# Reordering the list of pieces in a fused attention and SiLU layer

## The chip, the cores and the metric
The kernel runs on one core of a Trainium2 chip. The metric is the device time of one execution in microseconds (us). The five engines that matter are the TensorE (PE, with its weight loads shown as PEld), the VectorE (DVE), the ScalarE (ACT), the GpSimd (POOL) and the SyncE (SP), which issues nearly all of the transfers.

## What the kernel computes
The input is a sequence of 2048 rows of 512. It is layer-normed once (xn), and the output is `x + A(xn) + B(xn)`:

```python
# A: 32 heads of 16, four segments of 512 rows, an additive memory M, z between segments
logits = einsum('bhqd,bhkd->bhqk', qs, ks) * scale + mask        # inside one segment
a_dot  = einsum('bhqk,bhkd->bhqd', softmax(logits), vs)
a_mem  = (phi(qs) @ M) / (phi(qs) . z + 1e-6)                    # phi(t) = t+1 if t>0 else exp(t)
o      = g * a_mem + (1 - g) * a_dot                             # then o @ wo
M, z   = M + phi(ks)^T vs, z + sum(phi(ks))
# B: a dense layer with 1792 hidden columns
out    = silu(xn @ w1) @ w2
```

## The kernel before
The kernel is one list of pieces, `ORDER`, written out by hand or by a search: 1349 words, each of which calls one small function (the dictionary `PIECES` at the end of the kernel). The functions are run in the order of the list, and no scheduler moves an instruction afterwards. So the list sets the order of instructions on each engine's own queue; each engine works through its queue in that order, and waits where an operand isn't ready. A word before another in the list is not finished before it: only the queues, the buffers and the data hold it back.

The words that this document uses (s is a segment, 0 to 3; a segment is four tiles of 128 rows):

- `X t.1`, `Xv`, `Xa`: the first transposes of normed rows on PE, and the copies of them to `xnT` on DVE or ACT. `XD t`: the same for later tiles, as a transposing transfer from SP. `xs t` are the sums of the layer norm on DVE (L286, L289), `xg` the roots on POOL, and `Nv t` the normed rows (L315, on DVE).
- `k s.dt.part`, `q s.dt.part`, `v s.j.part`, `h s.ft.part`: parts of the products for keys, queries, values and hidden columns, on PE (L336, or L338 where the product is made of four strips of 32 columns). In segments 0 and 1 a tile has four parts, afterwards two. `kv`, `qv`, `vv` copy the finished tile out of its PSUM bank on DVE (L376, L399, L406); `ka`, `qa` do it on ACT. `kp` and `kf` split the keys by heads. `ha` is the tanh of a hidden tile on ACT (L492) and `hv` the product that follows on DVE (L497); `hv` is what empties the bank.
- `S t`: the scores of a batch (L724), at once followed on ACT by their exponentials `Pb` (L730) and on POOL by the causal mask (L744). There are 72 of them, and all write the same four PSUM banks, `psS`. So the scores of one batch can start only when the exponentials of the batch before have ended.
- `E n`, `O n`: weights times values (L791), for the even and odd heads; `Ev`, `Ov`, `Om` copy and merge the results on DVE and send the row sums on by small transfers (L813).
- `s`, `sv`, `r`, `w`, then `z`, `d` (small transfers from SP, L577, that spread a row to 16 partitions), `zv`, `dv`, `n`, `nv`: the normalization, and the memory's part. `fp`, `fa`, `fv` and `gp`, `ga`, `gv` form phi of keys and queries, `t` turns it by a transfer, `m`, `mv`, `mw` add it to the memory.
- `o`, `oc`, `od`, `oh` are parts of the output products (full, half and quarter width, and halves of the last tile); `xl` loads a tile of x, `st` and `sh` add it and store.

PSUM is the point where the queues hold each other. Four banks are `psS`. The other four are one pool:

```python
pp = ctx.enter_context(tc.tile_pool(name="pp", bufs=4, space=bass.MemoryType.PSUM))
psatt = ctx.enter_context(tc.tile_pool(name="psatt", bufs=1, space=bass.MemoryType.PSUM))
...
def bank(shape, dtype, name):
    return pp.tile(shape, dtype, name=name, tag="pb")
```

Every tile of k, q, v, h, the weighted values, the memory and most of the outputs takes one of these four banks with its first product, keeps it until its reader on DVE or ACT is done, and the next tile waits for that. With all four taken, the first product of a new tile waits for one particular reader, and so for everything that stands ahead of that reader on its queue.

A last rule in the driver makes a word's products in one piece or in four strips, after what stands around it, so that PE changes its way of tiling seldom: a dense word between two `S` takes strips if the next tiled word is an `E` or `O`. The list therefore sets this too.

Of the kernel before, what the change touches and what calls it, by code (L numbers as in the profile page):

```python
# [16 lines left out]
ones0 ones1 zeros xc0 xd0 xc1 xq0 xi0 Nv0 busy44 xd1 xq1 xc2 busy6 xi1 X0.1 xd2 xq2 Nv1 X1.1 Xa0.1 v0.0.0 v0.0.1 v0.0.2 xs3 xi2 Nv2 xq3 xi3 v0.0.3 X2.1 Xa1.1 k0.1.0 tb Nv3 X3.1 Xv2.1 k0.1.1 Xv3.1 vv0.0 odd omask k0.0.0 k0.0.1 k0.0.2 k0.0.3 ka0.0 fp0.0 q0.0.0 kf0.0 q0.0.1 q0.0.2 q0.0.3 k0.1.2 k0.1.3 q0.2.0 v0.2.0 qa0.0 xs5 ka0.1 kp0.1  # L17
S0 v0.1.0 v0.1.1 xs6 xs7 q0.2.1 v0.2.1 v0.2.2 v0.2.3 vv0.2 fa0.0 k0.2.0 k0.2.1 k0.2.2 xs4 xg4.4
S2 q0.2.2 q0.2.3 qv0.2 k0.2.3 kv0.2 fp0.2 fa0.2 v0.1.2 v0.1.3 vv0.1 Nv5 Nv6 XD6 q0.1.0 q0.1.1 q0.1.2 q0.1.3 qv0.1
S1 h0.0.0 h0.0.1 h0.0.2 xs10 h0.0.3 v0.3.0 v0.3.1 v0.3.2 v0.3.3 ha0.0 vv0.3 q0.3.0 kp0.2 hv0.0  # L20
# [4 lines left out]
S11 hv0.4 q1.2.0 q1.2.1 q1.2.2 v1.3.1 kind fa0.1 q1.2.3 qv1.2 v1.3.2 v1.3.3 vv1.3 Nv8 XD8 O0 lw0 kp0.3 fv0.0 Ov0
S6 fa0.3 k1.2.0 k1.2.1 k1.2.2 h0.5.0 h0.5.1 h0.5.2 q1.1.0 h0.5.3 ha0.5 k1.2.3 kv1.2 q1.1.1 q1.1.2 hv0.5
S8 h0.7.0 q1.1.3 qv1.1 h0.6.0 h0.6.1 h0.6.2 h0.6.3 ha0.6 fv0.3 E1 Ev1 k1.0.0
S9 hv0.6 h0.7.1 h0.7.2 h0.7.3 Om0 ha0.7 k1.0.1 k1.0.2 kp1.2 q1.0.0 q1.0.1 q1.0.2 fp0.1 Nv9 XD9 xs12 k1.0.3 kv1.0 kp1.0
# [3 lines left out]
S15 h1.10.0 h1.10.1 h1.10.2 hv0.10 kp1.1 xl0.2 h1.0.3 ha1.0 Nv11 XD11 E2 Ev2 O2 Ov2
S17 h1.10.3 k1.3.0 hv1.0 k1.3.1 k1.3.2 k1.3.3 kv1.3 fp1.3 h0.12.0 h0.12.1 xs14 m0.2 mv0.2 ha1.10 h0.12.2
S21 fv0.1 q1.3.0 q1.3.1 q1.3.2 q1.3.3 qv1.3 h1.3.0 hv1.10 gp1.1 h0.12.3 ha0.12 t0.1 h1.3.1 h1.3.2 t0.0 h1.3.3
S14 hv0.12 k2.2.0 h0.11.0 h0.11.1 k2.2.1 h0.11.2 h0.11.3 xl0.0 h0.13.0 ha1.3
S16 ha0.11 h0.13.1 h0.13.2 kp1.3 h0.13.3 xs13 kv2.2 hv1.3 ha0.13 q2.1.0 q2.1.1 qv2.1 E3
S19 Ev3 h1.11.0 h1.11.1 h1.11.2 h1.11.3 hv0.11 O3 hv0.13 fa1.3 k2.1.0 mw0.2 k2.1.1 Ov3 kv2.1 Om2
# [905 lines left out]
```

## Time and profile before

| | before |
|---|---|
| median of 3 runs | 220.42 us (219.86 to 220.8) |
| profiled execution, from first to last instruction | 218.2 us |
| PE, ACT, DVE, POOL busy in it | 210.9, 184.1, 181.3, 127.4 us |
| granted PE clock | 1.000 |
| exponentials of the 72 batches | 135.2 us, 1.878 us each |

The page gives no time of the profiled execution other than its span; 2.2 us lie between the span and the median of the runs. In the views, a line has the start, the length, the engine, the line of the kernel, the operation and the tiles (out<-in) and, in brackets, how long the engine sat idle before it and what ended that. PE's records overlap, since products are pipelined: the distance from one start to the next is what a product costs, not its length. A few of PE's records are missing (3982 of 4006 products), and each leaves a gap as long as a product.

### The profile page before, as it was taken

To read this page: it belongs to the slowest core of one execution; us is meant where nothing else is said; L and a number is where in the kernel's file an instruction comes from. 1 tells how busy PE (TensorE), PEld (TensorE's weight loads), DVE (VectorE), ACT (ScalarE), POOL (GpSimd) and SP (SyncE) were. 2 spreads that over 40 slices of the span, in tenths; PEclk is the share of its full clock that TensorE was granted. 3 is DMA by queue.
4 is the path that set the end of the run, shared out by engine and by line. 5 is a ranking of instruction groups with operands and counts; after the bars stand their busy time and mean duration, and the time that the engine had idled before them with its cause. 6 is when DMAs were issued, how large, how long until landed. Compare 5 with 4: busy or idle time off the path is not lost.

```text
span 218.2 us, 9267 instructions
## 1 busy us (share of the span) xinstructions
PE 210.9 (97%) x3982; PEld 116.1 (53%) x4006; DVE 181.3 (83%) x370; ACT 184.1 (84%) x173; POOL 127.4 (58%) x203
## 2 busy tenths in 40 slices
PE   7899999999999999999999999999999999999994
PEld 7666656655544544455444545445464544465653
DVE  6899999999799899667979886887979897858844
ACT  3799999999999999999999999999989998942000
POOL 6067676789568984697766436962787473410000
PEclk9999999999999999999999999999999999999999
DMA  6996249322200430541125131420042120412223
GB/s 183 344 375 160 51 125 243 74 53 53 51 5 17 157 71 10 117 95 40 49 67 83 54 97 28 74 77 6 0 132 73 52 73 13 131 32 79 84 66 98
DMA packets 33273, 19.60 MB, mean 90 GB/s; under 512 B 14672, under 2 KB 33232, under 8 KB 33232
## 3 DMA queue, kind: packets, MB, share of 16 engines
q1 hardware_dynamic: 30608, 16.39, 28.7%
q10 hardware_dynamic: 2624, 2.62, 3.8%
q8 instruction: 31, 0.51, 1.0%
q14 instruction: 10, 0.08, 0.1%
HBM read 9.96 MB, written 2.10 MB: 55 GB/s over the span
## 4 chain that ended last, share of the span: by engine, by line
PE 92%; DMA 3%; ACT 2%; issue 1%; SPq 1%; DVE 0%
PE ps L336 26%; PE psO L338 17%; PE ps L338 16%; PE psS L724 11%; PE psO L336 9%; PE psV L791 8%; PE psS L338 4%; DMA wk_sb<-in_A_wk_dram 3%; ACT Pb L730 2%; PE psM L452 1%; SPq L169 0%; SPq L158 0%; PE ps L509 0%; ACT th L492 0%; DVE o_half L668 0%
## 5 line engine op out<-in xcount | busy, mean ns | idle before, releaser
L730 ACT ACTIVATE Pb<-psS 128x2048 bf16<-128x2048 f32 x72 | 135.2, 1878 | 4.7 <-PE psS L724 2.4
L744 POOL TENSOR_SCALAR_AFFINE_SELECT Pb<-Pb 128x512 bf16<-128x512 bf16 (+2 forms) x88 | 62.3, 718 | 22.4 <-ACT Pb L730 19.6
L497 DVE SCALAR_TENSOR_TENSOR hT<-th,ps 128x512 bf16<-128x512 bf16 x56 | 38.0, 682 | 10.1 <-ACT th L492 9.4
L744 POOL TENSOR_SCALAR_AFFINE_SELECT lows<-Pb 64x512 bf16<-64x512 bf16 (+1 forms) x40 | 24.3, 607 | 32.0 <-ACT Pb L730 24.9
L338 PE MATMUL psO<-w_sb,hT 128*32 128x512 bf16 (+2 forms) x696 | 41.4, 321 | 0.0
L336 PE MATMUL ps<-xnT,w_sb 128*128 128x512 bf16 (+1 forms) x177 | 35.9, 330 | 0.2 <-issue 0.2
L492 ACT ACTIVATE th<-ps 128x512 bf16<-128x512 f32 x56 | 33.0, 594 | 3.5 <-PE ps L338 3.1
L338 PEld LDWEIGHTS <-hT 128*32 128x32 bf16 x864 | 21.5, 96 | 14.6 <-issue 3.1
L338 PE MATMUL ps<-xnT,w_sb 128*32 128x512 bf16 (+1 forms) x408 | 24.8, 349 | 0.0
L724 PE MATMUL psS<-qT,k 32*128 32x64 bf16 (+3 forms) x512 | 23.0, 233 | 0.2
L336 PEld LDWEIGHTS <-w_sb 128*128 128x128 bf16 x178 | 16.4, 98 | 11.9 <-issue 1.2
L336 PE MATMUL psO<-w_sb,hT 128*128 128x512 bf16 (+2 forms) x82 | 20.5, 324 | 0.7 <-issue 0.6
L791 PEld LDWEIGHTS <-Vz 128*32 128x32 bf16 x768 | 16.1, 97 | 9.5 <-issue 0.6
L791 PE MATMUL psV<-Pb,Vz 128*32 128x448 bf16 (+7 forms) x512 | 21.0, 286 | 0.0
L724 PEld LDWEIGHTS <-k 32*128 32x128 bf16 x512 | 9.3, 92 | 21.2 <-issue 20.4
L336 PE MATMUL ps<-xnT,wk_sb 128*128 128x256 bf16 (+1 forms) x63 | 14.4, 326 | 0.4 <-DMA wk_sb<-in_A_wk_dram 0.2
L724 PE MATMUL psS<-qT,kT 16*128 16x448 bf16 (+3 forms) x256 | 14.7, 269 | 0.0
L338 PEld LDWEIGHTS <-w_sb 128*32 128x32 bf16 x408 | 10.3, 96 | 6.7 <-issue 1.7
L621 DVE SCALAR_TENSOR_TENSOR o_out<-psO,x_res 128x512 bf16<-128x512 f32 x14 | 9.4, 679 | 5.0 <-PE psO L338 3.9
L336 PEld LDWEIGHTS <-hT 128*128 128x128 bf16 x92 | 8.5, 98 | 9.6 <-issue 2.1
L828 DVE CAST odd<-psV 128x512 bf16<-128x512 f32 x16 | 11.0, 687 | 2.4 <-PE psV L791 2.4
L338 PE MATMUL psO<-wo_sb,oT 128*32 128x512 bf16 x140 | 12.8, 379 | 0.0
(112 smaller groups left out, 330.0 us busy)
## 6 DMA issues: line engine op xcount, KB each, us to landing
spr<-rz SPq DMA_DIRECT2D x56, 64.0 KB
x_res<-in_A_x_dram SPq DMA_DIRECT2D x16, 128.0 KB
out_dram<-o_out SPq DMA_DIRECT2D x15, 128.0 KB
w_sb<-in_B_w_dram SPq DMA_DIRECT2D x2, 896.0 KB
w_sb<-in_B_w_dram ACTq DMA_DIRECT2D x1, 1792.0 KB
x_hi<-in_A_x_dram SPq DMA_DIRECT2D x2, 512.0 KB
wv_sb<-in_A_wv_dram SPq DMA_DIRECT2D x2, 256.0 KB
wk_sb<-in_A_wk_dram SPq DMA_DIRECT2D x1, 512.0 KB
```

The lines of the kernel that those rows point to most:

```text
L336: return [nc.tensor.matmul(out, lhsT=lhsT, rhs=rhs, start=start, stop=stop, skip_group_check=True)]
L338: nc.tensor.matmul(out[c : c + 32], lhsT=lhsT[:, c : c + 32], rhs=rhs, start=start, stop=stop, tile_position=(0, c), skip_group_check=True,)
L452: nc.tensor.matmul(psM[32 * g : 32 * g + 32, i, :].rearrange("p (r d) -> p r d", d=DH), lhsT=st["phiK", dt][:, j, 32 * g : 32 * g + 32], r ...
L492: nc.scalar.activation(out=th[:], in_=sts[s]["h", ft][:, :], func=AF.Tanh, scale=0.5)
L497: nc.vector.scalar_tensor_tensor(out=st["hT"][:, ft, :], in0=st.pop(("th", ft))[:], scalar=1.0, in1=st.pop(("h", ft))[:, :], op0=ALU.add, ...
L621: out = nc.vector.scalar_tensor_tensor(out=o_out[:], in0=st.pop(("psO", j)), scalar=0.5, in1=st["x", j][:], op0=ALU.mult, op1=ALU.add)
L724: nc.tensor.matmul(psS[:, g, c : c + q2 - q1], lhsT=keys[rows], rhs=st["qT"][rows, dt, q1:q2], start=True, stop=True, tile_position=(32 * ...
L730: exp = nc.scalar.activation(out=blocks(Pb, b).rearrange("p y g c -> p g y c"), in_=psS[:, :, :].rearrange("p g (y c) -> p g y c", c=BLOCK ...
L744: over[id(Pb)].append(nc.gpsimd.affine_select(out=out, in_=in_, compare_op=ALU.is_ge, fill=0.0, base=base, pattern=[[0, out.shape[1]], [1, ...
L791: nc.tensor.matmul(psV[32 * g : 32 * g + 32, q0 : q0 + nq].rearrange("p (y c) -> p y c", y=weights.shape[2]), lhsT=Vzs[s % 2][:, kt, 4 * d ...
L828: copy(out=odd[:], in_=sts[s].pop(("psV", 1))[:, :])
```

## The change
The words of `ORDER` behind the first transposes stand in another order. The words are the same 1349, and loads, buffers and functions are unchanged; 21 more PE instructions come from seven products that are now made in four strips rather than in one piece. Three lines of the list, early in the first segment, show what the change looks like (whole lines of the list, as the diff has them):

```diff
-S2 q0.2.2 q0.2.3 qv0.2 k0.2.3 kv0.2 fp0.2 fa0.2 v0.1.2 v0.1.3 vv0.1 Nv5 Nv6 XD6 q0.1.0 q0.1.1 q0.1.2 q0.1.3 qv0.1
-S1 h0.0.0 h0.0.1 h0.0.2 xs10 h0.0.3 v0.3.0 v0.3.1 v0.3.2 v0.3.3 ha0.0 vv0.3 q0.3.0 kp0.2 hv0.0
...
+S2 v0.1.1 vv0.2 v0.1.2 q0.2.2 v0.1.3 q0.2.3 kp0.1 qv0.2 fa0.2 q0.1.0 Nv6 vv0.1 q0.1.1 q0.1.2 h0.3.0
+S1 h0.3.1 q0.3.0 h0.3.2 omask Nv7 fp0.1 Nv5 h0.0.0 h0.0.1 q0.1.3 Nv4 XD6 h0.0.2 qv0.1 h0.0.3 ha0.0
+S3 v0.3.0 v0.3.1 xs11 h0.3.3 ha0.3 v0.3.2 v0.3.3 kp0.2 q0.3.1 hv0.0 xs10 q0.3.2 q0.3.3 k0.3.0
```

The first place is PE's queue at the third and fourth of the first transposes (`xn_t` through `ident`, into `ptr`). Rows with a minus stood there before, rows with a plus stand there now:

```order
 L845 LDWEIGHTS xn_t
 L845 MATMUL ptr<-ident,xn_t 128x128
-L336 LDWEIGHTS wk_sb
-L336 MATMUL ps<-xnT,wk_sb 128x256
-L336 LDWEIGHTS wk_sb
-L336 MATMUL ps<-xnT,wk_sb 128x256
 L845 LDWEIGHTS xn_t
 L845 MATMUL ptr<-ident,xn_t 128x128
```

Two half-width products with the key weights `wk_sb` no longer stand between the third and the fourth transpose; they come behind the fourth.

The second place is DVE's queue early in the first segment, from the last sums of tiles 4 to 7 to the copy of the second query tile. Before (`ps_304`, `ps_301`, `ps_344`, `ps_327`, `ps_387` are v0.2, q0.2, k0.2, v0.1 and q0.1):

```order
L406 CAST Vz0_111<-ps_304 128x16x2x16
L286 BN_STATS stats_351<-x_hi_79 128x6
L289 BN_AGGR mv_all_140<-stats_351 128x2
L399 CAST qT_306<-ps_301 128x512
L376 CAST kT_281<-ps_344 128x512
L406 CAST Vz0_111<-ps_327 128x16x2x16
L315 TENSOR_SCALAR xn_t_382<-x_hi_79,mv_all_140,rstd_all_141 128x512
L315 TENSOR_SCALAR xn_t_384<-x_hi_79,mv_all_140,rstd_all_141 128x512
L399 CAST qT_306<-ps_387 128x512
```

Now, on the same queue (`ps_327`, `ps_296`, `ps_300`, `ps_341`, `ps_378` are k0.2, v0.2, q0.2, v0.1 and q0.1):

```order
L286 BN_STATS stats_338<-x_hi_79 128x6
L289 BN_AGGR mv_all_140<-stats_338 128x2
L376 CAST kT_277<-ps_327 128x512
L406 CAST Vz0_111<-ps_296 128x16x2x16
L399 CAST qT_306<-ps_300 128x512
L315 TENSOR_SCALAR xn_t_381<-x_hi_79,mv_all_140,rstd_all_141 128x512
L406 CAST Vz0_111<-ps_341 128x16x2x16
L235 CAST omask_130<-pm_odd_122 128x1
L315 TENSOR_SCALAR xn_t_420<-x_hi_79,mv_all_140,rstd_all_141 128x512
L315 TENSOR_SCALAR xn_t_424<-x_hi_79,mv_all_140,rstd_all_141 128x512
L315 TENSOR_SCALAR xn_t_433<-x_hi_79,mv_all_140,rstd_all_141 128x512
L399 CAST qT_306<-ps_378 128x512
```

All four sums of tiles 4 to 7 stand ahead of the first copy now, one normed tile stands ahead of the copy of v0.1, and four of them with the small `omask`, where there were two, ahead of the copy of q0.1.

The third place is the end of DVE's queue. Before:

```order
L621 SCALAR_TENSOR_TENSOR o_out_5531<-psS_4936,x_res_5420 128x512
L668 SCALAR_TENSOR_TENSOR o_half_5554<-psS_4936,x_res_5466 128x256
L621 SCALAR_TENSOR_TENSOR o_out_5577<-psO_5154,x_res_4186 128x512
L668 SCALAR_TENSOR_TENSOR o_half_5604<-psS_4936,x_res_5466 128x256
L938 UNCONDITIONAL_BRANCH
```

Now:

```order
L621 SCALAR_TENSOR_TENSOR o_out_5564<-psO_5210,x_res_5332 128x512
L668 SCALAR_TENSOR_TENSOR o_half_5599<-psS_4973,x_res_5522 128x256
L621 SCALAR_TENSOR_TENSOR o_out_5602<-psO_5105,x_res_4904 128x512
L668 SCALAR_TENSOR_TENSOR o_half_5625<-psS_4973,x_res_5522 128x256
L938 UNCONDITIONAL_BRANCH
```

The four last additions are the same; in the list the word `sh1` (the first `o_half`) now stands directly ahead of `st3.1`, with five narrow products behind the two, where before the list had three full and two narrow products between them.

More of the change, by code (lines that the diff above doesn't have):

```diff
@@ L32 @@
[L32 to L37, printed above, removed]
@@ new lines @@
+S1 h0.3.1 q0.3.0 h0.3.2 omask Nv7 fp0.1 Nv5 h0.0.0 h0.0.1 q0.1.3 Nv4 XD6 h0.0.2 qv0.1 h0.0.3 ha0.0
+S3 v0.3.0 v0.3.1 xs11 h0.3.3 ha0.3 v0.3.2 v0.3.3 kp0.2 q0.3.1 hv0.0 xs10 q0.3.2 q0.3.3 k0.3.0
+S4 qv0.3 XD7 XD4 XD5 k0.3.1 k0.3.2 h0.2.0 h0.2.1 hv0.3 vv0.3 h0.2.2 k0.3.3 v1.2.0 h0.2.3 h0.1.0 ha0.2
+S7 h0.1.1 h0.1.2 h0.1.3 v1.2.1 fv0.0 v1.2.2 ha0.1 xs9 kv0.3 hv0.2 v1.2.3 E0 vv1.2 Ev0
+S5 lw0 v1.1.0 xs8 h0.4.0 v1.1.1 fp0.2 hv0.1 v1.1.2 v1.1.3 h0.4.1 h0.4.2 v1.3.0 vv1.1 h0.4.3
+S11 q1.2.0 O0 kind q1.2.1 v1.3.1 fa0.1 v1.3.2 q1.2.2 Ov0 fv0.2 q1.2.3 kp0.3 v1.3.3 ha0.4
@@ new lines @@
+S12 k1.1.0 vv1.0 h0.10.2 Nv11 h0.10.3 k1.1.1 k1.1.2 k1.1.3 ha0.10 Om0 h1.0.0 h1.0.1 hv0.9 h1.0.2
+S15 kv1.1 XD8 hv0.10 E2 h1.10.0 tanh h1.10.1 Ev2 h1.10.2 XD11 kp1.1 h1.0.3 ha1.0 O2
+S17 h1.10.3 k1.3.0 Ov2 k1.3.1 h0.12.0 k1.3.2 hv1.0 m0.2 mv0.2 k1.3.3 h0.12.1 ha1.10 t0.0 kv1.3
+S21 h0.12.2 h1.3.0 h0.12.3 q1.3.0 q1.3.1 h1.3.1 hv1.10 gp1.1 h1.3.2 t0.1 mw0.2 ha0.12 h0.11.0 xs15 h1.3.3
+S14 ha1.3 h0.11.1 h0.11.2 q1.3.2 q1.3.3 hv0.12 qv1.3 k2.2.0 k2.2.1 h0.11.3
+S16 q2.1.0 q2.1.1 hv1.3 kv2.2 qv2.1 ha0.11 h0.13.0 h0.13.1 fp1.3 fa1.3 Om2 h0.13.2 E3 h0.13.3
@@ new lines @@
+S26 q2.0.0 od0.2.11.1 hv1.1 q2.0.1 oc0.0.7.1 h1.7.0 gp1.0 h1.7.1 h1.7.2 h1.7.3 qv2.0 ha1.7 oc0.2.5.1
+S23 h1.4.0 zv0.2 h1.4.1 gv1.2 hv1.7 h1.4.2 o0.2.16 o0.0.8 h1.9.0 h1.4.3 od0.2.11.3 o0.2.13 z0.0 zv0.3 ha1.4 h1.9.1
+S25 o0.2.12 kp2.1 Om1 hv1.4 h1.9.2 o0.2.3 o0.2.17 fp1.2 E5 h1.9.3 ha1.9 oc0.0.2.0 Ev5 zv0.0 hv1.9 o0.0.16
+S29 k2.3.0 k2.3.1 o0.2.14 oc0.2.5.0 h1.2.0 h1.2.1 fa1.2 kp2.0 o0.0.17 oc0.0.2.1
+S27 zv0.1 kv2.3 O5 o0.0.9 h1.2.2 o0.0.14 h1.2.3 o0.2.15 oc0.2.10.0 o0.2.9 Ov5 ha1.2
+S31 h1.13.0 st0.2 hv1.2 h1.13.1 h1.13.2 h1.13.3 o0.3.8 fv1.2 ha1.13 Om5 Nv12 o0.3.9 o0.0.4 o0.3.14 o0.3.16 od0.3.3.2
@@ new lines @@
+S41 fa1.1 hv1.5 o0.1.1 mw0.0 o0.3.12 v2.3.0 oc0.3.2.1 O7 Ov7 v2.3.1
+S37 o0.1.5 vv2.3 fv1.1 q3.3.0 od0.1.8.2 fp2.0 q3.3.1 o0.1.10 s1 od0.1.8.3 o0.3.13 t1.0 od0.3.3.1 qv3.3 ga2.3 Om6 od0.1.8.1
+S36 st0.1 o0.3.5 Om7 k3.1.0 t1.1 k3.1.1 sv1 ka3.1 q3.1.0 q3.1.1 r1.3 od0.3.3.3
+S40 h1.6.0 r1.1 h1.6.1 r1.2 r1.0 fv2.0 w1 h2.8.0 h1.6.2 h1.6.3 z1.2 z1.0 o0.3.4 ha1.6 gp2.3 h2.8.1 oc0.3.2.0 qv3.1
+S43 o0.3.7 hv1.6 o0.3.6 o0.3.15 m1.0 o1.2.8 mv1.0 kp3.1 oc0.3.0.0 d1.2 o1.2.7 E8 st0.3 ha2.8
+S38 Ev8 fa2.2 oc1.2.11.0 hv2.8 zv1.0 z1.1 fp2.2 v3.0.0 o1.2.13 k3.0.0 v3.0.1 k3.0.1
```

113 lines of the change are left out of this document (48 added, 65 removed).

## Prediction
> **What bounds the kernel now.** I read the page first, then what PE waited for, then busy time by stage, and at last the order of time where the change starts.
>
> ```profile
> span 218.2 us, 9267 instructions
> PE 210.9 (97%) x3982; PEld 116.1 (53%) x4006; DVE 181.3 (83%) x370; ACT 184.1 (84%) x173; POOL 127.4 (58%) x203
> ...
> PE psS L864 <- DVE zraw L188: 1.1, 1, 1.1
> PE psO L336 <- issue: 1.0, 6, 0.2
> PE ptr L845 <- DVE xn_t L315: 0.5, 1, 0.5
> ...
> 0.00:11.95 11.95, 10.04 (x96) 8.32 (x98) 8.70 (x26) 6.82 (x16) 4.24 (x16) 1.00 0.84 274
> 11.95:28.70 16.75, 16.45 (x208) 10.69 (x212) 16.25 (x35) 16.69 (x16) 11.91 (x19) 1.00 0.58 167
> 28.70:58.26 29.56, 29.34 (x589) 17.17 (x593) 27.51 (x59) 28.98 (x26) 22.23 (x36) 1.00 0.46 111
> ```
>
> PE is busy 97% of the span, and once the transposes are through it waits for almost nothing: the longest waits in its list belong to the first 7 us, and the "issue" gaps of 0.2 us are as long as one product, so they are missing records. The stage rows (PE, PEld, DVE, ACT, POOL) add the second point: from 11.95 to 28.70 us PE, ACT and DVE are all full, DVE with 16.25 of 16.75 us. There a new order has no slack to use; whatever stands badly on DVE's queue must reach PE.
>
> Against the median of 220.42 us the sum is made in differences to this execution; the 2.2 us between span and median are carried over unchanged.
>
> **PE's own work** does not change:
>
> ```profile
> 185.60 0.86 PE ps L336 x4
> ...
> 188.49 0.86 PE ps L338 x16
> ```
>
> Four full products in one piece take 0.86 us, and so do sixteen strips, which are four products: 0.215 us each either way. The words are the same, and PE changes into the score tiling 72 times in both lists. So seven more products in strips cost 0, from 0 to +0.1.
>
> **The start** is the one place that gains.
>
> ```profile
> 7.96 0.41 DVE L315 TENSOR_SCALAR xn_t<-x_lo,mv_all,rstd_all 128x512 bf16<-128x512 bf16 x1
> 8.54 0.39 PE L336 MATMUL ps<-xnT,wk_sb 128*128 128x256 bf16 x2 [0.24 <-DMA wk_sb<-in_A_wk_dram]
> 8.77 0.39 PE L845 MATMUL ptr<-ident,xn_t 128*128 128x128 bf16 x4
> 9.19 0.42 DVE L851 COPY xnT<-ptr 128x512 bf16<-128x512 bf16 x1 [0.43 <-PE ptr L845]
> 10.11 1.04 PE L336 MATMUL ps<-xnT,wq_sb 128*128 128x256 bf16 x8
> 10.30 0.58 ACT L376 CAST kT<-ps 128x512 bf16<-128x512 f32 x1 [0.58 <-PE ps L336]
> 10.92 0.51 ACT L393 ACTIVATE k<-kT,pm_even 128x256 bf16<-128x256 bf16 x1
> 11.34 0.56 ACT L399 CAST qT<-ps 128x512 bf16<-128x512 f32 x1
> 11.95 0.21 PE L724 MATMUL psS<-qT,k 32*128 32x64 bf16 x4
> ```
>
> The fourth transpose stood behind key products that waited for `wk_sb` until 8.54. Now it needs only its normed tile, ready at 8.37 (7.96 + 0.41): it starts at 8.41, the key products follow at 8.64, and `xnT` is whole at 9.25 (0.42 to its copy, 0.42 for it). k0.0 ends after five quarter-tiles of 0.216 at 9.72, where it ended at 10.11. ACT's chain (10.30, 10.92, 11.34) moves with it: keys at 9.91, queries at 11.05 (q0.0 ends at 10.80, and a copy starts some 0.25 later), done at 11.61. PE has the same eleven quarter-tiles before the first scores and comes at 11.67. S0 starts at 11.68 instead of 11.95: **-0.27**, between 0 (if `wq_sb` lands only when it was first used, 10.11) and -0.35.
>
> **DVE's queue behind it** takes more than that away.
>
> ```profile
> 11.51 0.69 DVE L286 BATCH_NORM_STATS2 stats<-x_hi 128x6 f32<-128x512 bf16 x1 [0.23 <-DMA x_hi<-in_A_x_dram]
> 13.13 0.66 DVE L286 BATCH_NORM_STATS2 stats<-x_hi 128x6 f32<-128x512 bf16 x1
> 13.93 0.66 DVE L406 CAST Vz<-ps 128x512 bf16<-128x512 f32 x1
> 14.50 0.69 DVE L286 BATCH_NORM_STATS2 stats<-x_hi 128x6 f32<-128x512 bf16 x1
> 15.32 0.69 DVE L399 CAST qT<-ps 128x512 bf16<-128x512 f32 x1
> 15.93 0.68 DVE L376 CAST kT<-ps 128x512 bf16<-128x512 f32 x1
> 16.53 0.68 DVE L406 CAST Vz<-ps 128x512 bf16<-128x512 f32 x1
> 17.13 1.18 DVE L315 TENSOR_SCALAR xn_t<-x_hi,mv_all,rstd_all 128x512 bf16<-128x512 bf16 x2
> 18.22 0.68 DVE L399 CAST qT<-ps 128x512 bf16<-128x512 f32 x1
> ...
> 20.80 0.41 DVE L315 TENSOR_SCALAR xn_t<-x_hi,mv_all,rstd_all 128x512 bf16<-128x512 bf16 x1
> 22.01 1.88 ACT L730 ACTIVATE Pb<-psS 128x2048 bf16<-128x2048 f32 x1
> 23.93 0.40 PE L724 MATMUL psS<-qT,k 32*128 32x64 bf16 x8
> ```
>
> Starts give the prices: a pair of sums 0.82 (14.50 to 15.32), a copy 0.60, a normed tile 0.545 ((18.22 - 17.13) / 2). The queue can't start before `x_hi` lands at 11.51, and this transfer is not moved. In the new order: four pairs of sums to 14.75; k0.2, v0.2, q0.2 to 16.56; one normed tile and v0.1's copy from 17.11, ended at 17.79; `omask` and three normed tiles; q0.1's copy from 19.41 to 20.10.
>
> PE on its side needs banks. A batch of scores takes 0.39, and the next cannot start before 2.38 (0.45 to the exponentials, 1.88 for them, 0.05 back: 22.01 + 1.88 to 23.93). So S2 is at 14.06 and S1 at 16.44. Three quarter-tiles behind S1, at 17.48, h0.0 takes the bank of v0.1, which is freed at 17.82: it waits 0.34. Of this only 0.08 counts, since this stage has eight quarter-tiles (2.12 us) and would have waited for the exponentials; S3 is at 18.90. Directly behind S3, at 19.29, v0.3 takes the bank of q0.1, freed at 20.13: **0.84** (0.45 if the normed tiles cost 0.41 each, 1.0 if q0.1 slips further). Nine quarter-tiles later S4 starts at 22.08, against 21.55 in the trace. Its stage waits 0.1 for q0.3's copy, and S7, S5 and S11 follow at 24.52, 26.90 and 29.28. The trace has S11 at 28.70: +0.58. With a last wait of 0.1 at O0 for v1.1's copy I take **+0.65** at S6, the start's gain included; bounds +0.1 and +1.1.
>
> **Score stages further on.** A stage below 2.38 us of PE work waits for exponentials. The new list has 2.15 between S17 and S21 (seven quarter-tiles, one memory product, the scores): +0.23. Two short stages of the old list (2.33 ahead of S31 and 2.36 ahead of S40, by the same count of products) are full in the new one: -0.07. **+0.16**, 0 to +0.3.
>
> **Banks that come back late.** I counted, in both lists, first products that take a bank within 1.31 us of the last product of its former tile, where one DVE copy lies between: 21 now, 10 before. A copy needs about 1.05 (0.35 to start, 0.69), so each holds only if DVE is idle at that moment. At 0 to 0.1 us for each of the eleven more, and little for most: **+0.2**, 0 to +0.8.
>
> **The end.**
>
> ```profile
> 214.44 0.69 DVE L621 SCALAR_TENSOR_TENSOR o_out<-psO,x_res 128x512 bf16<-128x512 f32 x1 [0.17 <-PE psO L338]
> 214.98 0.28 PE L338 MATMUL psS<-wo_sb,oT 128*32 128x256 bf16 x4
> 215.31 0.42 DVE L668 SCALAR_TENSOR_TENSOR o_half<-psS,x_res 128x256 bf16<-128x256 f32 x1 [0.18 <-PE psS L338]
> ```
>
> The last addition starts 0.33 behind the last product. Now a half addition (0.42) and a full one (0.69) run back to back ahead of it; they start 0.81 before the last product and end 0.33 behind it. They just fit, and the full tile's store goes out some 0.2 later: **+0.05**, 0 to +0.2.
>
> Sum: 0.65 + 0.16 + 0.2 + 0.05 = +1.06, so 220.42 + 1.06 = **221.5 us**.
>
> **The rivals.** A measurement of this kernel tells 0.5% (1.1 us) from no change.
>
> *x_hi lands early* (no change, 0.17). The 11.51 is one execution's landing. If the sums start at 10.9, when DVE is free, the chain is 0.6 earlier, h0.0 waits for nothing, v0.3 waits 0.24, and S11 comes at about 28.65: -0.05 + 0.16 + 0.1 + 0.05 gives 220.7. Against it: DVE's wait for the transfer is in the trace.
>
> *Small transfers were the cost* (faster, 0.07). If the timed runs have waits for late `spr` rows on the path that the profile has off it, the new list can remove them.
>
> ```profile
> DVE oT L589 <- DMA spr<-rz: 0.9, 2, 0.5
> ```
>
> With these 0.9 us, the start's 0.27 and the 0.07 above all gained, and no late bank, it gives 219.2. It decides from the point where such a wait of DVE holds PE; in the trace PE has none behind it, and the first spread, z0.2, is now read after 4.9 us of PE work where it was 7.7.
>
> *Transfers with too short a lead* (slower, 0.08). The list issues d2.2 2.6 us of PE work before it is read (7.5 before), and the transpose of tile 12 3.4 us before q3.3 (23.6 before). Each late by 0.6 (an estimate: the wait for `spr` above is 0.5 each) adds 1.2: 222.7.
>
> *POOL holds DVE's normed tiles* (slower, 0.08).
>
> ```profile
> 17.53 0.63 POOL L417 TENSOR_SCALAR pos<-kT 128x512 bf16<-128x512 bf16 x1
> 22.86 0.38 DVE L315 TENSOR_SCALAR xn_t<-x_hi,mv_all,rstd_all 128x512 bf16<-128x512 bf16 x1
> ```
>
> The two normed tiles at 17.13 took 1.18 beside this work of POOL, the one at 22.86 took 0.38. If each of the three tiles ahead of q0.1 waits out one POOL instruction (0.63) and then takes 0.38, they cost 1.01 each instead of 0.545: +1.4, 222.9. Against it: the two in the trace cost less than 2 x 1.01. The Trainium skill's page "SBUF — State Buffer", section "Who interferes with whom", states such a rule: a DVE tensor_scalar in a two-port mode and a GpSimd instruction exclude each other for the whole instruction. By that rule the sum would be this rival's 222.9, by the row it is 221.5; the trace agrees that the two disturb each other, but shows 0.21 more per tile (1.18/2 - 0.38) and not a whole POOL instruction.
>
> **How the numbers follow.** The sum's case has 0.60; its own range is 220.7 to 222.4, since most of its unknowns only add, and a little over half of it (0.34) lies beyond 221.5. So slower by over 0.5% has 0.34 + 0.16 = 0.50; within 0.5% has 0.26 + 0.17 = 0.43; faster has 0.07. The range that leaves out the faster case and the upper parts of the two slow rivals is 220.1 to 222.8.
>
> **What would show it.** S0 near 11.7 us. On PE a wait of some 0.8 us for DVE's copy of q0.1 (L399) directly behind the fourth batch of scores, and a shorter one before it for L406. S11 near 29.3. A wait for Pb of about 0.2 at S21. PE's busy time stays near 211 us. I am wrong if v0.3's first product follows S3 without a gap, or if PE waits for a transfer in the later segments.

## The result, and the profile after

| | before | after |
|---|---|---|
| median of six runs | 220.40 us | 226.75 us |
| ratio, with 95% interval | 1 | 1.0285 (1.0258 to 1.0312) |
| profiled execution, its span | 218.2 us | 224.6 us (run time 226.35) |

One of the six runs after, 229.98 us, was in the chip's slower state and is not in the ratio; the median of the other five is 226.36 us. The new order is 6.3 us slower, outside the range of 220.1 to 222.8 that was forecast. On the page of the kernel after, the span, the busy time of the engines and the shares of the chain that ended last:

```profile
span 224.6 us, 9318 instructions
...
PE 215.2 (96%) x4027; PEld 116.2 (52%) x4027; DVE 182.0 (81%) x370; ACT 184.2 (82%) x173; POOL 127.9 (57%) x203
...
PE 64%; DVE 15%; issue 6%; DMA 4%; POOL 4%; ACT 3%; SPq 2%; DVEq 0%; ACTq 0%; POOLq 0%
```

The same line of shares on the page of the kernel before:

```profile
PE 92%; DMA 3%; ACT 2%; issue 1%; SPq 1%; DVE 0%
```

Busy times hardly differ: DVE has 0.7 us more, ACT 0.1. (PE's 4.3 more are mostly records: 24 are missing before and none after. The old list without masks, experiment e7 below, has all 4006 records and 214.2 us, so some 3.3 are records.) But the chain, which ran over PE for 92%, now goes over DVE for 15% and over POOL for 4%. PE waits for them. The seven longest waits behind 12 us in the list of PE's waits after (us, count, mean):

```profile
PE ps L338 <- DVE qT L399: 0.8, 1, 0.8
PE ps L336 <- DVE hT L497: 0.5, 1, 0.5
PE ps L338 <- DVE oT L608: 0.5, 1, 0.5
PE ps L336 <- DVE qT L399: 0.5, 1, 0.5
PE ps L338 <- DVE oraw L821: 0.4, 1, 0.4
PE ps L336 <- DVE omask L235: 0.4, 1, 0.4
PE psV L791 <- POOL Pb L744: 0.3, 1, 0.3
```

Where the loss arises is seen from the starts of some batches of scores (rows of L724) in the two traces:

| | S0 | S6 | S19 | S36 | S59 | S71 | last product | end |
|---|---|---|---|---|---|---|---|---|
| before, us | 11.95 | 31.21 | 58.26 | 104.88 | 161.65 | 189.99 | 214.98 | 218.24 |
| after, us | 11.90 | 32.08 | 59.72 | 108.08 | 166.90 | 196.27 | 220.83 | 224.64 |
| difference | -0.05 | +0.87 | +1.46 | +3.20 | +5.25 | +6.28 | +5.85 | +6.40 |

It grows up to S71; only 0.87 us of it lies in the first stretch, on which the prediction had spent most of its working.

For the rest I went through PE's starts. Behind 12 us, the new list has 18 places where the distance from one start to the next is over 0.06 us longer than that pair of products needs elsewhere. They make 6.15 us; the old list has four, 0.46 us. (Missing records are left out.) Two early ones make 1.13: h0.0 at 18.26, v0.3 at 20.34. Five late ones make 3.39: O4 at 73.71, h1.9 at 79.74, v2.3 at 103.98, q3.0 at 124.56, v3.1 at 140.03. Eleven between 0.07 and 0.27 make 1.63.

The longest, 0.96 us, shows the kind. PE, DVE and POOL of the kernel after around it:

```profile
123.55 0.24 PE L338 MATMUL psO<-w_sb,hT 128*32 128x128 bf16 x4
124.56 0.62 PE L338 MATMUL ps<-xnT,wq_sb 128*32 128x512 bf16 x8 [0.78 <-DVE qT L399]
```

```profile
120.92 0.69 DVE L497 SCALAR_TENSOR_TENSOR hT<-th,ps 128x512 bf16<-128x512 bf16 x1 [1.05 <-ACT th L492]
121.52 1.10 DVE L599 TENSOR_TENSOR phiQT<-spr,phiQT 128x512 bf16<-128x512 bf16 x1
122.55 0.41 DVE L472 TENSOR_TENSOR Mbf<-M,bmask 128x256 bf16<-128x256 f32 x1
122.88 0.50 DVE L479 TENSOR_TENSOR Zw<-b,z 128x16 bf16<-128x16 f32 x2
123.28 0.63 DVE L589 TENSOR_TENSOR oT<-spr,oraw 128x512 bf16<-128x512 bf16 x1
123.83 0.68 DVE L399 CAST qT<-ps 128x512 bf16<-128x512 f32 x1
```

```profile
121.25 1.09 POOL L744 TENSOR_SCALAR_AFFINE_SELECT Pb<-Pb 128x1024 bf16<-128x1024 bf16 x1
122.84 0.80 POOL L744 TENSOR_SCALAR_AFFINE_SELECT Pb<-Pb 128x256 bf16<-128x256 bf16 x2 [0.50 <-ACT Pb L730]
```

q3.0 takes the bank of q3.2. Its reader is the copy at 123.83, and three words stand ahead of it on DVE: dv1.2, mw1.2 (two kinds of rows) and zv1.2. The second thing to see is their length. dv1.2 (L599) takes 0.42 where POOL is idle, here 1.10: it began while a causal mask ran on POOL from 121.25 to 122.34, and ended 0.28 behind that mask's end.

That is the rule in both traces. Of the L589 and L599 that began with over 0.15 us of a POOL instruction still to run, 19 of 20 ended 0.27 to 0.28 behind its end, however much was left of it. (In the one exception, before, the two began within 0.01 us of each other, and POOL's instruction was the longer one: 0.89 instead of 0.61.) All 12 of L315 that began with over 0.26 us to run ended 0.14 to 0.15 behind it. The copies out of PSUM (L399, L406, L821) take 0.63 to 0.69 with and without POOL. I call this a hold. Over all of DVE's instructions that can be held (L315, L433, L468, L472, L479, L550, L589, L599, L835), the time above the unheld kind is 8.7 us before and 11.2 after (to some 0.5, by which unheld length is taken).

### The profile page after: what moved, and what is told of

Same layout as the page of the kernel before. It is cut to its first block, busy times and chain, and to the rows that moved or that the text cites. A ratio compares the mean times of both kernels' runs of the same rounds, so it can differ in the third digit from the quotient of the medians.

```text
span 224.6 us, 9318 instructions
## 1 busy us (share of the span) xinstructions
PE 215.2 (96%) x4027; PEld 116.2 (52%) x4027; DVE 182.0 (81%) x370; ACT 184.2 (82%) x173; POOL 127.9 (57%) x203
## 4 chain that ended last, share of the span: by engine, by line
PE 64%; DVE 15%; issue 6%; DMA 4%; POOL 4%; ACT 3%; SPq 2%; DVEq 0%; ACTq 0%; POOLq 0%
PE ps L336 17%; PE psO L338 13%; PE ps L338 11%; PE psS L724 7%; PE psV L791 6%; PE psO L336 5%; DMA x_hi<-in_A_x_dram 3%; PE psS L338 3%; DVE phiQT L599 2%; ACT Pb L730 2%; DVE hT L497 2%; POOL Pb L744 2%; DVE phiQT L433 1%; ACT th L492 1%; DVE oT L589 1%
## 5 line engine op out<-in xcount | busy, mean ns | idle before, releaser
L338 PE MATMUL psO<-w_sb,hT 128*32 128x512 bf16 (+2 forms) x704 | 45.3, 326 | 0.0
L336 PE MATMUL ps<-xnT,w_sb 128*128 128x512 bf16 (+1 forms) x177 | 38.5, 330 | 1.1 <-DVE hT L497 0.5
L338 PE MATMUL ps<-xnT,w_sb 128*32 128x512 bf16 (+1 forms) x412 | 26.1, 349 | 0.0
L724 PE MATMUL psS<-qT,k 32*128 32x64 bf16 (+3 forms) x512 | 23.0, 233 | 0.1
L336 PE MATMUL psO<-w_sb,hT 128*128 128x512 bf16 (+2 forms) x90 | 22.0, 320 | 0.0
L724 PEld LDWEIGHTS <-k 32*128 32x128 bf16 x512 | 9.2, 92 | 20.8 <-issue 20.1
L336 PE MATMUL ps<-xnT,wk_sb 128*128 128x512 bf16 (+1 forms) x67 | 14.9, 329 | 0.0
L724 PE MATMUL psS<-qT,kT 16*128 16x448 bf16 (+3 forms) x256 | 14.7, 269 | 0.0
L338 PE MATMUL psO<-wo_sb,oT 128*32 128x512 bf16 x156 | 14.4, 380 | 0.1
L336 PE MATMUL ps<-wv_sb,xnT 128*128 128x512 bf16 x42 | 12.7, 380 | 0.5 <-DVE qT L399 0.5
```

Of the source, the lines that this page charges most:

```text
L336: return [nc.tensor.matmul(out, lhsT=lhsT, rhs=rhs, start=start, stop=stop, skip_group_check=True)]
L338: nc.tensor.matmul(out[c : c + 32], lhsT=lhsT[:, c : c + 32], rhs=rhs, start=start, stop=stop, tile_position=(0, c), skip_group_check=True,)
L724: nc.tensor.matmul(psS[:, g, c : c + q2 - q1], lhsT=keys[rows], rhs=st["qT"][rows, dt, q1:q2], start=True, stop=True, tile_position=(32 * ...
```

## The experiments

The table has the waits of PE behind 12 us in the profiled execution, counted as above, and the sum of DVE's lengthening. Each kernel was timed against the kernel before on the same chip (medians 220.1 to 220.5); three have a single run, and so no interval. In the profiled execution of e1 the products between 25 and 28 us took about twice as long as elsewhere (0.21 for a half-width product of 0.108), so its waits aren't summed.

| kernel | median, us | ratio (95%) | PE's waits, us | DVE longer by, us |
|---|---|---|---|---|
| before | 220.4 | 1 | 0.46 | 8.7 |
| after | 226.75 | 1.0285 (1.0258 to 1.0312) | 6.15 | 11.2 |
| e1, early words moved | 228.43 | 1.0377 (1.0320 to 1.0435) | - | 12.2 |
| e2, late words moved behind | 225.31 | 1.0210 (1.0166 to 1.0253) | 4.68 | 10.3 |
| e3, e1 and e2 | 226.10 | 1.0283 (1.0213 to 1.0353) | 5.61 | 10.8 |
| e4, new list to S6, then the old | 222.75 | 1.0098 (1.0062 to 1.0134) | 3.34 | 9.0 |
| e5, three words in the old list | 222.04 | 1.0080 (1.0057 to 1.0103) | 1.92 | 10.1 |
| e6, after without masks | 223.34 | single run | 2.58 | 3.5 |
| e7, before without masks | 220.61 | single run | 0.35 | 2.2 |
| e8, late words into idle time | 225.47 | 1.0237 (1.0182 to 1.0293) | 3.12 | 9.2 |
| e9, e8 with the old head | 225.15 | 1.0206 (1.0157 to 1.0255) | 4.12 | 7.9 |
| e10, e5 without masks | 220.49 | single run | 0.52 | 2.5 |
| e11, e8 with XD12 earlier | 224.64 | 1.0197 (1.0169 to 1.0225) | 3.90 | 8.6 |
| e12, e9 with XD12 earlier | 223.26 | 1.0135 (1.0104 to 1.0166) | 3.06 | 8.4 |

**First theory: each wait is the price of one misplaced word.** Then a move of a few words takes it away.

```diff
-S2 ... q0.1.0 Nv6 vv0.1 q0.1.1 q0.1.2 h0.3.0
-S1 h0.3.1 q0.3.0 h0.3.2 omask Nv7 fp0.1 Nv5 h0.0.0 h0.0.1 q0.1.3 Nv4 XD6 h0.0.2 qv0.1 h0.0.3 ha0.0
+S2 ... q0.1.0 vv0.1 Nv6 q0.1.1 q0.1.2 h0.3.0
+S1 h0.3.1 q0.3.0 h0.3.2 fp0.1 h0.0.0 h0.0.1 q0.1.3 XD6 h0.0.2 qv0.1 omask Nv7 Nv5 Nv4 h0.0.3 ha0.0
```

> The new list, with five words of DVE moved in its first 21 us: the normed tile Nv6 behind the copy vv0.1, and omask, Nv7, Nv5, Nv4 behind the copy qv0.1. In the trace of the new list h0.0 waits 0.56 us for vv0.1's bank at 18.26 and v0.3 waits 0.57 us for qv0.1's bank at 20.34. Theory A (each stall is the price of one word that stands ahead of a bank's reader on DVE): both go, 226.7 - 1.1 = 225.6, between 225.3 and 226.0. Rival B (the queue behind is as full, and the late normed tiles or late copies give the time back further on): over 226.3. Rival C (the loss is in small transfers that come late): no change.

It became slower, 228.4, and its interval lies clear of the new list's. Both early waits are gone, and a longer one stands behind them. DVE and PE of this kernel:

```profile
19.93 2.23 DVE L315 TENSOR_SCALAR xn_t<-x_hi,mv_all,rstd_all 128x512 bf16<-128x512 bf16 x3
22.08 0.68 DVE L286 BATCH_NORM_STATS2 stats<-x_hi 128x6 f32<-128x512 bf16 x1
22.79 0.18 DVE L289 BATCH_NORM_AGGREGATE mv_all<-stats 128x2 f32<-128x6 f32 x1
22.89 0.66 DVE L497 SCALAR_TENSOR_TENSOR hT<-th,ps 128x512 bf16<-128x512 bf16 x1
```

```profile
23.60 0.38 PE L336 MATMUL ps<-xnT,wk_sb 128*128 128x256 bf16 x2 [1.57 <-DVE hT L497]
```

The three normed tiles took 1.51 in the new list. Here the last of them meets a mask, they take 2.23, and PE waits 1.73 us for the next bank's reader, the product of h0.0. Rival B holds in this stretch: its queue has no free time.

```diff
-S18 ... xl0.0 kv2.0
-S22 o0.0.3 v2.2.0 ga1.0 h1.1.0 xg12.4 h1.1.1 ...
+S18 ... xl0.0 kv2.0 xg12.4
+S22 o0.0.3 v2.2.0 ga1.0 h1.1.0 h1.1.1 ...
...
-S23 h1.4.0 zv0.2 h1.4.1 gv1.2 hv1.7 h1.4.2 ...
+S23 h1.4.0 zv0.2 h1.4.1 hv1.7 gv1.2 h1.4.2 ...
...
-S34 ... vv2.0 gv1.3 E7 XD12 ha1.5 o0.1.7 oc0.1.9.0 Ev7
+S34 ... vv2.0 E7 XD12 ha1.5 o0.1.7 oc0.1.9.0 Ev7 gv1.3
...
-S39 ... q3.2.0 dv1.2 v3.3.0 mw1.2 zv1.2 q3.2.1 qv3.2 v3.3.1 ...
+S39 ... q3.2.0 dv1.2 v3.3.0 q3.2.1 qv3.2 mw1.2 zv1.2 v3.3.1 ...
...
-S49 ... od1.0.1.0 dv1.0 o1.0.16 n1.1 o1.0.0 nv1.1 o1.0.3
+S49 ... od1.0.1.0 o1.0.16 n1.1 o1.0.0 nv1.1 dv1.0 o1.0.3
```

> The new list, with six words moved at five places behind 60 us: xg12.4 ahead of S22, gv1.2 behind hv1.7, gv1.3 behind Ev7, mw1.2 and zv1.2 behind qv3.2, dv1.0 behind nv1.1. The trace of the new list has PE waiting there 0.46, 0.69, 0.58, 0.96 and 0.70 us, 3.4 together. Theory A: nearly all of it goes, 226.7 - 3.1 = 223.6, between 223.2 and 224.3. Rival B (a queue without slack: what is moved behind makes the next reader late): less than half goes, over 225.2. Rival C (transfers): no change.

> The eleven moves of the two runs before together. Theory A: the two gains add, 222.5, between 222.0 and 223.2; what is left over the kernel before is the dozen of waits under 0.3 us. Rival B: the gains overlap or turn into new waits, over 224.5.

Of the 3.4 us, 1.4 came back in the time. The first two of the five waits are gone, the other three were replaced by waits of 0.54, 0.66 and 0.34 and a new one of 0.21. At q3.0's place, on DVE and PE of e2:

```profile
123.52 0.84 DVE L589 TENSOR_TENSOR oT<-spr,oraw 128x512 bf16<-128x512 bf16 x1
124.28 0.68 DVE L821 CAST oraw<-psV 128x512 bf16<-128x512 f32 x1
```

```profile
125.01 0.62 PE L791 MATMUL psV<-Pb,Vz 128*32 128x448 bf16 x16 [0.48 <-DVE oraw L821]
```

zv1.2, moved behind the copy of q3.2, now stands ahead of the next bank's reader, and is held there (0.84 instead of 0.41). e3 adds the early moves to this; its median is 0.8 above e2's, but the intervals of the two ratios overlap. The first theory falls: a word's move pays only where the queue behind it has room.

**The head alone, and one bad place alone.**

The first kernel is a splice: the new list up to S6, then the old list's words in their order. At the seam the words that the new head has already run (fp0.1) are left out, and those that it has not run yet (tanh of xg8.4, fp0.3, hv0.4, qv1.2, vv1.3, Nv8, XD8) are put in. The second kernel moves three words in the old list.

> The new list up to S6 (its first 185 words), then the remaining words in the old order. It prices alone the stretch for which the prediction worked out +0.65 us, and which in the two traces costs +0.87 (S6 at 32.08 against 31.21). Theory A: 220.4 + 0.87 = 221.3, between 221.0 and 221.6. Rival B (the old list further on has slack that takes the delay up): 220.4 to 220.8. Rival D (a bad head also makes the rest worse, since DVE stays behind): over 222.

222.75: rival D, by its bound of 222. Besides the 0.87 up to S6, PE waits 0.60 at 33.66 and 0.46 at 36.73, directly behind the seam, where DVE is still behind. A further 0.80 at 177.99 follows a wait of DVE of 0.9 us for a late `spr` row in this execution (0.5 in the trace before); without it the time would be near 222.0, at that bound, so this run alone does not decide for D. The times lie between 221.9 and 223.4.

```diff
-S42 ... vv3.0 zv1.1 gv2.3 o1.2.4 fp2.2 zv1.2
-S39 hv2.11 q3.2.0 ga2.1 q3.2.1 qv3.2 d1.0 v3.3.0 ...
-S44 dv1.2 q3.0.0 q3.0.1 Ev9 mw1.0 oc1.2.3.1 ...
+S42 ... vv3.0 zv1.1 gv2.3 o1.2.4 fp2.2
+S39 hv2.11 q3.2.0 ga2.1 q3.2.1 dv1.2 mw1.0 zv1.2 qv3.2 d1.0 v3.3.0 ...
+S44 q3.0.0 q3.0.1 Ev9 oc1.2.3.1 ...
```

> The old list with three words moved: dv1.2, mw1.0 and zv1.2 now stand directly ahead of the copy qv3.2 on DVE, as the like words do in the new list at its longest stall (0.96 us, q3.0 waiting for the bank of q3.2). Nothing else changes. Theory A (one such order is enough, in a list with no other fault): +0.5 to +1.0, 220.9 to 221.4. Rival B (the old list's slack takes it up; the stalls need a list that is behind everywhere): within 0.2 of 220.4.

222.04, 1.9 us above the kernel before on that chip: more than theory A's upper end. One wait arises, of 1.45 us, at q3.0. DVE and PE:

```profile
117.33 0.69 DVE L497 SCALAR_TENSOR_TENSOR hT<-th,ps 128x512 bf16<-128x512 bf16 x1 [0.52 <-ACT th L492]
117.93 1.09 DVE L599 TENSOR_TENSOR phiQT<-spr,phiQT 128x512 bf16<-128x512 bf16 x1
118.95 0.83 DVE L472 TENSOR_TENSOR Mbf<-M,bmask 128x256 bf16<-128x256 f32 x1
119.70 0.47 DVE L479 TENSOR_TENSOR Zw<-b,z 128x16 bf16<-128x16 f32 x2
120.08 0.62 DVE L589 TENSOR_TENSOR oT<-spr,oraw 128x512 bf16<-128x512 bf16 x1
120.63 0.68 DVE L399 CAST qT<-ps 128x512 bf16<-128x512 f32 x1
```

```profile
121.36 0.83 PE L338 MATMUL ps<-xnT,wq_sb 128*32 128x512 bf16 x12 [1.38 <-DVE qT L399]
```

**Order or hold.** The same kernels without most of the masks tell the two apart.

```diff
-            over[id(Pb)].append(nc.gpsimd.affine_select(
+            (nc.gpsimd.affine_select(
...
-            for first in chunks:
-                select(first[:, :, 0:HP], first[:, :, 0:HP], HP)
             return
...
-        select(firsts[:, :, 0:P], firsts[:, :, 0:P], 0)
```

The first pair of lines stops the remaining masks from being put on the list of what later exponentials wait for.

> The new list without the causal masks of the weights Pb (the 88 POOL instructions Pb<-Pb of L744 are left out, so the weights above the diagonal aren't zeroed; those that fill lows stay). In the trace of the new list the DVE instructions that read and write bf16 tiles in SBUF (L315, L433, L589, L599, L835 and a few more) are 11.2 us longer together than their shortest kind, 6.7 of it while such a mask runs. Theory E (DVE instructions of this kind are held until POOL's is through, and these held ones make the bank's reader late): L599 and L589 beside nothing fall to 0.42, the 11.2 fall to about 4.5, and the time by 2.5 to 3.5 us, to 223.2 to 224.2. Rival F (the order of words alone makes the reader late, the holds fall in slack): the time falls by under 1 us.

> The old list without the same 88 masks. Here 8.7 us of lengthened DVE instructions, 6.4 of them beside such masks, reach PE nowhere. Theory E: DVE's busy time falls by 5 to 6.5 us and the time by under 0.4, to 220.0 to 220.5. Rival F: the same small change; it differs from E only in the new list.

> e5_one_bad (three words moved in the old list, one stall of 1.45 us) without the same 88 causal masks as in the two kernels without masks. In e5 the words between hv2.11 and the bank's return took 1.09, 0.83, 0.47, 0.62 and 0.68 us; at their shortest (0.42, 0.41, 0.28, 0.41, 0.68) the copy would end 1.4 us sooner. Theory E (the stall is mostly the hold by POOL): a stall of 0 to 0.4 at this place. Rival F (the order alone): 1.0 or more.

The new list falls by 3.0 to 3.4 us (by the median of the five runs or of all six) to 223.34, the old one doesn't fall (220.61), and the one bad place costs nothing any more (220.49). DVE and PE of e10, at the same place (line numbers behind the edit are 3 smaller):

```profile
117.80 0.69 DVE L497 SCALAR_TENSOR_TENSOR hT<-th,ps 128x512 bf16<-128x512 bf16 x1 [0.58 <-ACT th L492]
118.40 0.64 DVE L599 TENSOR_TENSOR phiQT<-spr,phiQT 128x512 bf16<-128x512 bf16 x1
118.97 0.41 DVE L472 TENSOR_TENSOR Mbf<-M,bmask 128x256 bf16<-128x256 f32 x1
119.30 0.27 DVE L479 TENSOR_TENSOR Zw<-b,z 128x16 bf16<-128x16 f32 x2
119.47 0.41 DVE L589 TENSOR_TENSOR oT<-spr,oraw 128x512 bf16<-128x512 bf16 x1
119.81 0.68 DVE L399 CAST qT<-ps 128x512 bf16<-128x512 f32 x1
```

```profile
120.54 0.83 PE L338 MATMUL ps<-xnT,wq_sb 128*32 128x512 bf16 x12
```

The order is that of e5 word for word; the copy begins 2.01 us behind the start of hv2.11 instead of 3.30, and the wait falls from 1.45 to 0.17. So at this place the hold is nearly all of the price.

In the whole of the new list PE's waits fall from 6.15 to 2.58, but this is not the hold alone, because the masks also stand in POOL's own queue. Of the five long waits, three have held DVE instructions ahead of the late reader (h1.9, q3.0, v3.1; 2.35 us together). O4 (0.46) waits for a mask itself, and v2.3 (0.57) stands behind a DVE instruction that waited for a result of POOL:

```profile
102.63 0.69 DVE L433 SCALAR_TENSOR_TENSOR phiQT<-ex,pos 128x512 bf16<-128x512 bf16 x1 [1.65 <-POOL pos L417]
```

That L417 began at 101.99, directly behind masks in POOL's queue; in e6 this wait of DVE is gone. How the 3.6 us divide between the hold and POOL's queue is measured only at q3.0's place. Nor are the 2.58 that remain the order's alone: 1.05 of them stand where DVE idled 1.32 us for a late `spr` row (178.94), a place that costs 0.26 in the new list's profile. Without this wait and the 0.35 of the old list without masks, about 1.2 us are left for the order, beside the masks that e6 keeps (its DVE is still lengthened by 3.5). The Trainium skill's page "SBUF — State Buffer", section "Who interferes with whom", states that a DVE instruction with two SBUF inputs contends with a GpSimd instruction that reads SBUF, and that the order of issue decides which of the two blocks. The trace agrees: the later L599 ends 0.27 behind POOL's instruction.

**Moves into idle time.** Before hv2.11 DVE sat idle for 1.05 us (the row at 120.92), and for 0.65 before hv2.12. Words moved there go ahead of the bank's reader without delaying it. Besides the first two moves of e2 (xg12.4 and gv1.2):

```diff
-S39 gv2.3 hv2.11 ... dv1.2 ... mw1.2 zv1.2 q3.2.1 qv3.2 ...
+S39 gv2.3 dv1.2 mw1.2 hv2.11 ... q3.2.1 qv3.2 ...
...
+S44 ... Ev9 zv1.2 q3.0.0 ...
+S46 ... dv1.0 hv2.12 ...
+S41 fa1.1 hv1.5 gv1.3 ...
```

> The new list with the five late places mended in another way than in e2_late_mended: words go where the trace of the new list has DVE idle, ahead of the bank's reader, or behind every reader that PE needs soon. xg12.4 ahead of S22 and gv1.2 behind hv1.7 as there; gv1.3 behind hv1.5 (not between Ev7 and it); dv1.2 and mw1.2 ahead of hv2.11 (DVE idle 1.05 us before it); zv1.2 behind Ev9; dv1.0 ahead of hv2.12 (idle 0.65 before it). Theory G (DVE has free time near each place, and what is moved into it costs nothing): 226.7 - 3.0 = 223.7, between 223.3 and 224.4. Rival B (any move returns about half, as in e2_late_mended with 225.3): 224.8 to 225.6.

> The list of e8_idle_slots with its words up to S6 in the old order. Theory G: the two early stalls go as well, 0.9 less, 222.8, between 222.3 and 223.5. Rival D (a seam costs what it saves, as behind S6 in e4_new_head): 223.7 or more.

By the trace theory G holds: from S0 to S71 the profiled execution of e8 takes 181.3 us, where the new list takes 184.4, which is the 3.0 expected, and the five late waits are below 0.15 each. The median, 225.47, is rival B's, and the interval of the ratio overlaps the new list's, so the time shows no gain clear of noise. Part of that is in the start (S0 at 12.59 in this execution, with a wait for `wk_sb`), and the four times lie apart, 224.2 to 226.6. e9's median, 225.15, misses theory G's 222.8 and lies over rival D's bound of 223.7 too. Its profiled execution shows one source. PE and SP:

```profile
106.11 0.62 PE L338 MATMUL ps<-xnT,wq_sb 128*32 128x512 bf16 x8 [1.72 <-DVE pk L433]
```

```profile
101.78 1.20 SPq L857 DMA_TRANSPOSE xnT<-xn_t x1
```

q3.3 waits 1.91 us. The DVE instruction named had ended at 105.37; the product's other wait is for the transposes of `xnT`, the last of which, XD12, was issued at 101.78. PE was ready for it at 104.20, 2.42 behind 101.78. In e8 the same product came 2.64 behind, in the new list 3.49, and neither waited. But 15 of XD12's 16 parts had landed by 104.48, and the last only at 106.02. So 0.28 of the 1.91 at most is the shorter lead, and the rest is one late part. What held that part up was not tested; one packet of instructions ran on a DMA queue in that time (104.01 to 104.96).

```diff
-S34 ... E7 XD12 ha1.5 ...
...
+S31 ... Nv12 XD12 ...
```

> The list of e8_idle_slots, with one more move: XD12, the transposing transfer of tile 12, directly behind Nv12, where its rows are ready, some 9 us earlier. In the profile of e9_old_head_idle PE waits 1.91 us at q3.3, the first product that needs tile 12, with the transfer issued 4.3 us before; the profile of e8_idle_slots has no such wait, and its four times lie 2.4 us apart (224.2 to 226.6). Theory H (this transfer has too short a lead, and is late in some executions): the times draw together at the lower end, median 224.2, between 223.6 and 224.6, and none over 225. Rival I (the spread has other sources, such as the loads of the start): median 225.0 to 225.8, spread over 2 us as before.

> The list of e9_old_head_idle with the same move of XD12. Theory H: without the wait of 1.91 us, median 223.3, between 222.7 and 223.8, which is the price of everything that still differs from the old list behind S6 (a wait of 0.5 us at the seam and a dozen below 0.35). Rival I: 224.5 to 225.5.

e12 came out at 223.26, as theory H had it. In e11 the times drew together (224.4 to 225.4 instead of 224.2 to 226.6), but the median, 224.64, is just above theory H's range (223.6 to 224.6), and one run lies over 225. In both a new wait of 0.8 us stands at m1.2. PE of e11:

```profile
97.32 0.38 PE L452 MATMUL psM<-Vz,phiK 128*32 128x32 bf16 x32 [0.63 <-DMA phiK<-pk]
```

It waits for the transposing transfer of phi, and again for one part: 15 of 16 had landed by 96.48, the last at 97.28. Whether XD12, moved ahead on the same queue, made it late was not separated. The eleven small waits were not mended one by one either. No run points to a list faster than the old one, which leaves PE 0.46 us of waits and gains nothing from the loss of the masks.

## Why the prediction was wrong, point by point

- **What bounds the kernel.** PE, 97%: right, and PE's work did stay the same. That there is no slack early was right too. But the loss was looked for there: 0.87 of 6.4 us arises before S6.
- **The start, -0.27.** Measured -0.05. The transposes moved as described, but `x_lo` landed 0.07 later, the first key products began at 8.73 instead of 8.64, and S0 followed the full eleven quarter-tiles with 0.1 more.
- **DVE's queue early, +0.65 at S6, bounds +0.1 to +1.1.** Measured +0.87. Waits of 0.34 and 0.84 were forecast at h0.0 and v0.3; they are 0.56 and 0.57. The first normed tile waited for POOL's root (DVE idled 0.29 until 16.90) and was then held itself (0.70), so v0.1's copy began at 17.53 and not at 17.11. The rows of PE after:

```profile
18.26 0.60 PE L336 MATMUL ps<-xnT,w_sb 128*128 128x256 bf16 x4 [0.40 <-DVE omask L235]
...
20.34 0.38 PE L336 MATMUL ps<-wv_sb,xnT 128*128 128x512 bf16 x1 [0.50 <-DVE qT L399]
```

- **Score stages, +0.16.** About right: S21 waits 0.16 for its exponentials.
- **Banks that come back late, +0.2, 0 to +0.8. This is the step that failed.** PE's waits behind the first two make 5.0 us, some 4 of them late banks (O4's 0.46 is a mask, S21's 0.16 the exponentials, and some small ones were not traced). Two things were wrong in it. The criterion compared the time between a bank's last product and its next first product with one copy of 1.05 us, and so took note only of places below 1.31. Of the five long waits one was among those 21 (v2.3, 1.29). v3.1 has 1.40, q3.0 1.68 and h1.9 1.83, by the same count; O4 waits for a mask on POOL. What has to fit into this time is the reader with everything that stands ahead of it on DVE. And the price, 0 to 0.1 each, left the hold out, which lengthens one such instruction by up to 0.8; at one such place alone PE waited 1.45 us with the masks and 0.17 without most of them (e5 and e10).
- **The end, +0.05, 0 to +0.2.** The additions were said to fit just in time. They didn't: the first waits for PE until 220.61, and the two behind it run on from there. The last addition starts 0.72 behind the last product's start (220.83) instead of 0.33, and the end, with its store, comes 0.55 us later than it did:

```profile
220.61 0.42 DVE L668 SCALAR_TENSOR_TENSOR o_half<-psS,x_res 128x256 bf16<-128x256 f32 x1 [0.18 <-PE psS L338]
220.96 0.68 DVE L621 SCALAR_TENSOR_TENSOR o_out<-psO,x_res 128x512 bf16<-128x512 f32 x1
221.55 0.41 DVE L668 SCALAR_TENSOR_TENSOR o_half<-psS,x_res 128x256 bf16<-128x256 f32 x1
```

- **The rival that POOL holds DVE (0.08, 222.9)** had the right mechanism, and was priced at three normed tiles instead of at all of DVE's held instructions. The row that spoke against it was misread. Behind the 1.18 of the two tiles at 17.13 are two held tiles. Each waited out an instruction of POOL, the first a mask that the prediction did not show, the second the L417 of 17.53, which ended at 18.16. The mask and the two tiles, before:

```profile
16.88 0.66 POOL L744 TENSOR_SCALAR_AFFINE_SELECT Pb<-Pb 128x512 bf16<-128x512 bf16 x1
```

```profile
17.13 0.57 DVE L315 TENSOR_SCALAR xn_t<-x_hi,mv_all,rstd_all 128x512 bf16<-128x512 bf16 x1
```

```profile
17.61 0.69 DVE L315 TENSOR_SCALAR xn_t<-x_hi,mv_all,rstd_all 128x512 bf16<-128x512 bf16 x1
```

The tiles ended at 17.70 and 18.30, both about 0.15 behind the end of POOL's instruction. So a held tile costs what is left of POOL's instruction and these 0.15, and not a whole instruction and its own 0.38 on top. The rival's 1.01 for each tile was too much, the row did not speak against the hold, and the sum's 0.545 was a held price already. The three tiles ahead of q0.1 took 1.43 (0.48 each) in the new list.
- **x_hi early (0.17).** The sums of `x_hi` did begin early, at 11.10 instead of 11.51, and it saved nothing: the first normed tile waited for POOL's root, and h0.0 waited 0.56 all the same.
- **Small transfers as the cost (0.07).** DVE's 0.9 us of waits for `spr` are gone in the new list's profile, and the time went up. But a late `spr` row did cost PE 1.05 us in the profiled executions of e1 and e6. **Too short a lead (0.08)**: no such wait in the new list. XD12's came out in e9, 1.91 us where 0.6 was allowed; at most 0.28 of it is the lead, the rest one late part of the transfer.

## What to carry to other kernels

Where PE is full and its banks come back through another engine, compare the time that each bank is free for with the whole queue ahead of its reader, at the lengths that these instructions have beside POOL, and not with the reader alone. Compare the end of an instruction with the end of POOL's instruction beside it: its length alone hides the rule, since a held one can be anything from a little to a whole POOL instruction longer. Holds need not cost much: the old list's DVE instructions are lengthened by 8.7 us, and its PE waits for 0.46. Mend a new list by moves into idle time, judge by the time as well as by the waits (e8's waits fell by 3.0 us, its time by no more than the noise), and expect a move behind a reader to fall on the next.

## What the hardware showed that was not expected

- The hold is whole and has a fixed remainder: 0.27 to 0.28 us behind the end of POOL's instruction for a `TENSOR_TENSOR` of 128x512 bf16 in SBUF (19 of 20), 0.14 to 0.15 for `TENSOR_SCALAR` (12 of 12), in the traces before and after. L599 without masks and with them, in the rows of the one line, of e6 and of after (shortest, median and longest in ns):

```profile
L599 DVE TENSOR_TENSOR phiQT<-spr,phiQT x12: 363/418/643, 119.0 to 204.9; 128x512 bf16<-128x512 bf16 x12
```

```profile
L599 DVE TENSOR_TENSOR phiQT<-spr,phiQT x12: 361/459/1198, 121.5 to 208.0; 128x512 bf16<-128x512 bf16 x12
```

- It works the other way too: POOL's L385 (128x512) takes 0.69 at its shortest and up to 1.20 after, L417 0.61 and up to 1.04.
- One part of a small transfer can land long behind the others: in e9 15 of the 16 parts of a transpose that was issued at 101.78 had landed by 104.48, the last at 106.02, and the product that reads it waited 1.91 us. The same was seen in e11 (97.28 against 96.48) and, for a `spr` row, in e4 (7 parts by 173.81, the last at 175.86); why is open.
